# Maxima over partitions through TensorE instead of GpSimd, and dense queries in the two halves of the array

## The chip, the cores and the metric

The kernel runs on one core of one Trainium2 chip. A core has TensorE (PE: matrix products; PEld is its weight load), VectorE (DVE), ScalarE (ACT), GpSimd (POOL) and SyncE (SP, which issues most DMAs). Each engine works through its own queue in order and waits for the others by semaphores. The metric is the device time of one execution in microseconds.

## The reference

Three steps follow each other: attention with a window and four sink positions, a routed layer of eight experts, each of which takes exactly 192 tokens, and a dense two-layer network with a leaky activation.

```python
scores = scale * np.matmul(q, k.transpose(0, 1, 3, 2))     # q, k, v: (2, 8, 768, 64)
keep = is_sink | in_window                                 # 4 sinks, window of 128
scores = np.where(keep, scores, -1000000000.0)
a = np.exp(scores - np.max(scores, axis=-1, keepdims=True))
a = a / (np.sum(a, axis=-1, keepdims=True) + 1e-09)
x = np.matmul(a, v)                                        # then (1536, 512)

logits = x @ w_gate                                        # (1536, 8)
for idx in np.argsort(-logits.flatten()):                  # best pair first
    tok, e = idx // 8, idx % 8
    if assigned[tok] >= 0 or counts[e] >= 192: continue
    assigned[tok] = e; counts[e] += 1
out[assigned == e] = np.maximum(x[assigned == e] @ w1[e], 0.0) @ w2[e]    # w1: (512, 1024)

h = out @ w_in                                             # (1536, 512) @ (512, 2048)
return (np.maximum(h, 0.0) + alpha * np.minimum(h, 0.0)) @ w_out
```

## The kernel before

The program is written as a list of tasks, each with the engines that could do it, an assumed duration, the buffers it reads and writes, and what it must follow. A planner (`Plan.run`) goes through that list in simulated time: of the tasks that could start it takes the one that starts first, by rank where they tie, fixes its engine and takes its buffers from their rings. The order on each engine, and the choice of engine where there are two, come from these assumed durations; the chip only keeps the order. The planner assumes 0.42 or 0.48 us for a reduction over partitions on GpSimd. `boost` raises a task's rank.

**Attention.** Twelve blocks of 128 queries (two batches of six), in each four pairs of heads. `qk` makes the scores of a pair: for each head one product of 128 rows, with the head's 64 rows of queries in a stationary tile whose other 64 rows are zeros (`qT` is laid out that way, 512 KB per block), against the keys of both heads, 130 or 260 columns. The scores go to four banks, the ring `s`. VectorE masks them and takes the row's minimum (`soft`, L451), ScalarE takes the exponential (`expo`, L462), TensorE turns P (`transp`, L476), ScalarE and VectorE split it in two halves of 16 bits (`hilo`, L485, L486), and TensorE multiplies with V (`pv`, L527 to L535), four to seven steps later. V too is split, after it was scaled by a power of two: `vmax` takes the largest |v| of each partition, `vscale` combines the blocks of a batch (L375), and `pow2_scale` takes the maximum over all 128 partitions and makes the scale and its inverse from the exponent bits. The maximum is a `partition_all_reduce` on GpSimd (L356). `pow2_scale` runs three times, for each batch and for the gate's weights. `prep_v` then splits V on GpSimd (`vh` L405, scaled V L407, `vl` L409), for the first block on ScalarE and VectorE.

**Routing.** Eight experts close one after another. `closing` counts, for every pair of token and expert, how many tokens stand ahead of it (masks `cm` on VectorE, ScalarE or GpSimd, L966 to L985; counts on TensorE, L1017). From these `thresholds` finds per partition and expert the key of the last token that fits (`red`, L1031), and `total` takes the maximum over partitions, again a `partition_all_reduce` on GpSimd (`tot`, L1034). `close` (`name`, L896 to L900) picks the expert with the highest key, `ranks` (L1049) numbers its tokens. Seven closings do this; the eighth expert takes what is left. Then one-hot tiles `ohs` (L1114) give the token numbers (L1231), GpSimd gathers the rows by indirect DMA (`xg`, L1250) and TensorE turns them (L1263, 128 and 64 rows in turn).

**Experts and chunks.** Two experts (L1345 to L1352) and then one chunk of the dense network with their 384 tokens (`lay1` L1419, `lay2` L1441), four times over. Operands are split in a high part (`spl`, L1297, and `gt`, L1428, on ScalarE) and a low part (L1288, on GpSimd or VectorE). The dense weights are converted to 32 bits along the way (L765 to L776).

The closings run beside the experts and chunks of the step before. What the change touches most are these lines:

```python
m2 = cst.tile([128, 1], F32, name="m2" + name)
task({"POOL": 0.42}, lambda: nc.gpsimd.partition_all_reduce(m2, m1[0], 128, ...ReduceOp.max), r=[m1[1]], w=[a])   # L356
...
def total():
    nc.gpsimd.partition_all_reduce(tot.tile, red.tile, 128, ...ReduceOp.max)      # L1034
```

## Time and profile before

| | before |
|---|---|
| median of 3 runs | 765.0 us (764.94 to 768.23) |
| profiled execution | 766.29 us, span 764.6 us |
| mean granted TensorE clock | 0.888 |
| busy: PE, PEld | 625.8 us (82%), 547.6 us (72%) |
| busy: DVE, ACT, POOL | 535.1 us (70%), 391.3 us (51%), 398.0 us (52%) |
| DMA | 79.24 MB, mean 104 GB/s |
| reductions over partitions on GpSimd | 3 at L356 (first at 19.8 us), 7 at L1034 (142.5 to 571.3 us) |

In a timeline row stand the start and the length in us, engine, line, operation and tiles, and in brackets how long the engine was idle before it and what ended that; "issue" there means that nothing the profile shows ended it. In a row of the waits stand who waited for whom, the sum in us, the number of times and the longest. PE's time is the time that its instructions are in the array, so that overlapping ones count once.

### The profile page before, as it was taken

The numbers are of one execution on the slowest core, as the hardware profiler recorded it, in microseconds if no ns is written. First come the engines' busy times: TensorE is split into PE (matmuls) and PEld (weight loads), VectorE is DVE, ScalarE is ACT, GpSimd is POOL, SyncE is SP. The second block draws the span as 40 slices with busy tenths as digits, with TensorE's granted clock in tenths as the row PEclk, the third lists the DMA queues.
The fourth block names the chain that finished last, engine by engine and source line by source line (L and its number), as shares of the span: only waits on it lengthen the run. The fifth ranks groups of instructions, "written<-read, shape, count | busy, mean of one in ns | idle before, by whom it ended". The sixth has DMA issues, their size and how long they took to land.

```text
span 764.6 us, 12677 instructions
## 1 busy us (share of the span) xinstructions
PE 625.8 (82%) x4473; PEld 547.6 (72%) x4474; DVE 535.1 (70%) x1225; ACT 391.3 (51%) x865; POOL 398.0 (52%) x425
## 2 busy tenths in 40 slices
PE   5559997749699577768989995949786999989996
PEld 4448886438598466557888874739785988888995
DVE  5548889749577799956888875627964655886651
ACT  6448887324363466324775342317634444775452
POOL 4526744242431566426766654337645556766563
PEclk9579997559889799778999998879998999999998
DMA  8835433515773453102740003016402002730001
GB/s 252 261 97 135 129 72 74 191 51 189 252 252 107 137 166 98 48 28 60 212 157 1 3 22 121 29 48 219 158 1 83 1 22 83 223 122 1 1 1 42
DMA packets 40283, 79.24 MB, mean 104 GB/s; under 512 B 15518, under 2 KB 22204, under 8 KB 40124
## 3 DMA queue, kind: packets, MB, share of 16 engines
q1 hardware_dynamic: 37916, 71.60, 29.9%
q0 software_dynamic: 2304, 6.84, 2.7%
q8 instruction: 35, 0.57, 0.3%
q14 instruction: 28, 0.23, 0.1%
HBM read 69.45 MB, written 6.36 MB: 99 GB/s over the span
## 4 chain that ended last, share of the span: by engine, by line
PE 38%; DVE 24%; issue 10%; ACT 5%; DMA 4%; POOL 3%; POOLq 0%; ACTq 0%; DVEq 0%; SPq 0%
PE o L1441 12%; PE h L1419 12%; DVE cm L970 4%; PE h L1345 4%; DVE spl L1288 3%; DVE ohs L1114 2%; DVE v L1426 2%; PE h L1352 2%; PE r L1263 2%; DVE w L769 2%; ACT spl L1297 2%; DVE h L1337 2%; PE h L1347 2%; DMA xg<-xd,sidx 2%; DMA raw<-w 1%
## 5 line engine op out<-in xcount | busy, mean ns | idle before, releaser
L1441 PE MATMUL o<-spl,gt 128*128 128x512 f32 x576 | 162.0, 425 | 37.6 <-POOL gt L1288 24.0
L1288 POOL TENSOR_TENSOR spl<-w,spl 128x512 fp32r<-128x512 f32 x81 | 113.0, 1399 | 90.1 <-ACT spl L1297 52.3
L1441 PEld LDWEIGHTS o<-spl,gt 128*128 128x128 f32 x576 | 112.5, 203 | 64.3 <-POOL gt L1288 28.0
L1419 PE MATMUL h<-x,spl 128*128 128x384 f32 x768 | 151.7, 348 | 1.7 <-POOL x L1288 0.7
L1419 PEld LDWEIGHTS h<-x,spl 128*128 128x128 f32 x768 | 141.7, 196 | 8.0 <-DVE x L1288 1.2
L1288 POOL TENSOR_TENSOR spl<-raw,spl 128x512 fp32r<-128x512 f32 x57 | 76.2, 1343 | 43.1 <-ACT spl L1297 23.1
L1426 DVE SCALAR_TENSOR_TENSOR v<-t,nal,v 128x384 f32<-128x384 f32 x64 | 70.0, 1094 | 21.5 <-ACT t L1424 20.5
L1288 POOL TENSOR_TENSOR gt<-v,gt 128x384 fp32r<-128x384 f32 x50 | 55.5, 1111 | 46.3 <-ACT gt L1428 39.3
L1297 ACT CAST spl<-w 128x512 fp32r<-128x512 f32 x94 | 57.8, 619 | 33.4 <-PE o L1441 17.7
L1428 ACT CAST gt<-v 128x384 fp32r<-128x384 f32 x64 | 32.8, 513 | 80.5 <-DVE v L1426 79.3
L1345 PE MATMUL h<-xT,spl 128*128 128x384 f32 x192 | 59.2, 373 | 10.5 <-DVE jt L1333 10.5
L1297 ACT CAST spl<-raw 128x512 fp32r<-128x512 f32 x92 | 55.4, 619 | 16.8 <-PE o L1441 6.1
L1288 DVE TENSOR_TENSOR spl<-w,spl 128x512 fp32r<-128x512 f32 x47 | 42.2, 898 | 26.4 <-ACT spl L1297 26.1
L1345 PE MATMUL h<-h,spl 128*128 128x384 f32 x192 | 56.3, 362 | 3.1 <-DVE h L1337 1.7
L1423 ACT ACTIVATE v<-h 128x384 f32<-128x384 f32 x64 | 31.3, 489 | 51.3 <-PE h L1419 45.9
L442 PE MATMUL s<-k,q 128*128 128x260 f32 (+1 forms) x192 | 53.3, 408 | 3.9 <-DMA q<-qT 3.8
L970 DVE TENSOR_SCALAR cm<-mrow,m 128x384 bf16<-128x384 f32 (+10 forms) x85 | 55.2, 685 | 1.6 <-ACT mrow L955 1.6
L1288 DVE TENSOR_TENSOR spl<-raw,spl 128x512 fp32r<-128x512 f32 x39 | 39.8, 1022 | 20.5 <-ACT spl L1297 19.9
L1017 PEld LDWEIGHTS <-cm 128*128 128x128 bf16 x684 | 24.2, 100 | 41.3 <-DVE cm L970 32.6
L462 ACT ACTIVATE P<-sm,mn 128x260 f32<-128x260 f32 (+1 forms) x96 | 43.6, 489 | 11.1 <-DVE mn L451 10.8
L1347 PE MATMUL h<-xT,spl 128*128 128x192 f32 x192 | 49.0, 255 | 0.0
L1347 PE MATMUL h<-h,spl 128*128 128x192 f32 x192 | 48.1, 251 | 0.0
(199 smaller groups left out, 1344.2 us busy)
## 6 DMA issues: line engine op xcount, KB each, us to landing
raw<-w SPq DMA_DIRECT2D x64, 512.0 KB, 3.9
r<-w_in SPq DMA_DIRECT2D x16, 512.0 KB, 3.4
r<-w_out SPq DMA_DIRECT2D x16, 512.0 KB, 3.9
q<-qT SPq DMA_DIRECT2D x11, 512.0 KB, 9.5
vraw<-v SPq DMA_DIRECT2D x4, 768.0 KB, 8.2
xd<-x SPq DMA_DIRECT2D x12, 256.0 KB, 2.4
k<-kT SPq DMA_DIRECT2D x11, 260.0 KB, 4.4
mrow<-md SPq DMA_DIRECT2D x3, 384.0 KB, 3.1
```

Source lines behind the costliest of these rows:

```text
L442: nc.tensor.matmul(s.tile[:, :n], lhsT=qs[t].tile[:, p, a], rhs=kk, start=True, stop=True)
L462: task({"ACT": act(n) + 0.137}, lambda h=h, sm=sm, mn=mn: nc.scalar.activation(P[t].tile[:, h, :n], sm.tile[:, :n], AF.Exp, bias=mn.tile, ...
L970: nc.vector.tensor_scalar(cm.tile[:, x:y], mrow[:, x:y], m.tile[:, c1:c1 + 1], None, op)
L1288: eng.tensor_tensor(*aps(), OP.subtract)
L1297: (nc.scalar.copy if e == "ACT" else nc.vector.tensor_copy)(b.tile[:, 0], get())
L1345: nc.tensor.matmul(ps.tile[:, 0:2 * CAP], lhsT=w[:, 0, k], rhs=x.rearrange("p a t -> p (a t)"), start=first and k == 0, stop=False, skip_g ...
L1347: nc.tensor.matmul(ps.tile[:, CAP:2 * CAP], lhsT=w[:, 1, k], rhs=x[:, 0], start=False, stop=last and k == len(xs) - 1, skip_group_check=True)
L1419: nc.tensor.matmul(ps.tile[:, 0:CH], lhsT=w[:, i, k], rhs=x[:, j], start=(k == n == 0), stop=(k == KD - 1 and n == 2))
L1423: task({"ACT": act(CH)}, lambda: nc.scalar.activation(v.tile, ps.tile[:, 0:CH], AF.Relu), r=[ps], w=[v])
L1426: task({"DVE": dve(CH) + 0.065}, lambda: nc.vector.scalar_tensor_tensor(v.tile, t.tile, nal[:, f:f + 1], v.tile, OP.mult, OP.add), r=[t, n ...
L1428: task({"ACT": act_sb(CH)}, lambda: nc.scalar.copy(gt.tile[:, 0], v.tile), r=[v], w=[gt.part(0)])
L1441: nc.tensor.matmul(ops[t].tile, lhsT=gt.tile[:, i, sl], rhs=wo.tile[:, j], start=(f == n == 0), stop=(f == FB - 1 and n == 2))
```

## The change

Three things are changed.

First, no maximum over partitions is on GpSimd any more. In `pow2_scale` TensorE turns the 128 maxima into one row in a bank of the ring `s`, VectorE takes the row's maximum, TensorE spreads it back over 128 partitions (a transpose of the value repeated 128 times), and the four small operations read it from the bank. These tasks get a `boost` of 40. In `closing` the same is done for eight experts at once: `red` (128 x 8) is turned to 8 x 128 in free columns of the bank that holds the counts, VectorE takes eight maxima (`tot`, now 8 x 1), and a second transpose gives 128 x 8; `close` reads that from the bank.

Second, the queries are dense: `qT` holds the two heads of a pair in partitions 0 to 63 and 64 to 127 and no zeros (256 KB per block), and each head's product takes its own half: 64 rows of queries against 64 rows of keys. Both products of a pair are one task, with two banks.

Third, the planner, asked whether a task with several new buffers of one ring can start, looks for as many free ones (`free_at(n)`).

```diff
-    def free_at(self):
-        return self.pick()[0]
+    def free_at(self, n=0):
+        if not n:
+            return self.pick()[0]
+        at = []
+        for old in self.past:
+            if old is None:
+                at.append(0.0)
+            elif all(t.start is not None for t in old.users):
+                at.append(max((t.end for t in old.users), default=0.0))
+        return sorted(at)[n] if len(at) > n else None
...
-                            f = b.ring.free_at()
+                            f = b.ring.free_at(asked.count(b.ring))
+                            asked.append(b.ring)
...
+EAGER = 40.0
...
-    r_q, r_P = ring("q", [128, NP, 2, 128], F32, 4), ring("P", [128, H, 2 * KW], F32, 2)
+    r_q, r_P = ring("q", [128, NP, 128], F32, 4), ring("P", [128, H, 2 * KW], F32, 2)
...
     def pow2_scale(m1, name):
-        m2 = cst.tile([128, 1], F32, name="m2" + name)
+        m2 = cst.tile([128, 2], F32, name="m2" + name)
         o = cst.tile([128, 4], I32, name="sc" + name)
-        a, b = Res(), Res()
+        a, b, c, ps = Res(), Res(), Res(), r_s.new()
         def power():
-            nc.vector.tensor_scalar(m2, m2, 1.0e-30, None, OP.max)
-            nc.vector.tensor_scalar(o[:, 0:1], m2.bitcast(I32), 0x7F800000, None, OP.bitwise_and)
+            nc.vector.tensor_scalar(m2[:, 0:1], ps.tile[:, 128:129], 1.0e-30, None, OP.max)
+            nc.vector.tensor_scalar(o[:, 0:1], m2[:, 0:1].bitcast(I32), 0x7F800000, None, OP.bitwise_and)
...
-        task({"POOL": 0.42}, lambda: nc.gpsimd.partition_all_reduce(m2, m1[0], 128, bass.bass_isa.ReduceOp.max),
-             r=[m1[1]], w=[a])
-        task({"DVE": 0.6}, power, r=[a], w=[b])
+        task({"PE": 0.12}, lambda: nc.tensor.transpose(ps.tile[0:1, 0:128], m1[0], ident), r=[m1[1]], w=[ps.part(0)], boost=EAGER)
+        task({"DVE": 0.2}, lambda: nc.vector.tensor_reduce(m2[0:1, 1:2], ps.tile[0:1, 0:128], AX.X, OP.max),
+             r=[ps.part(0)], w=[a], boost=EAGER)
+        task({"PE": 0.12}, lambda: nc.tensor.transpose(ps.tile[:, 128:129], m2[0:1, 1:2].to_broadcast([1, 128]), ident[0:1, 0:1]),
+             r=[a], w=[ps.part(1)], boost=EAGER)
+        task({"DVE": 0.6}, power, r=[ps.part(1)], w=[b], boost=EAGER)
...
     def qk(t, p):
         b, i, j0, n = geo(t)
-        for a in range(2):
-            s = S[t, p, a] = r_s.new()
-            def fn(a=a, s=s):
-                kk = kall[:, b, p].rearrange("p j k -> p (j k)")[:, j0 * KW:j0 * KW + n]
-                nc.tensor.matmul(s.tile[:, :n], lhsT=qs[t].tile[:, p, a], rhs=kk, start=True, stop=True)
-            qks.append(pe(n / 599.0 + 0.012, fn, [...], [s]))
+        ss = [r_s.new() for _ in range(2)]
+        S[t, p, 0], S[t, p, 1] = ss
+        def fn():
+            for a, s in enumerate(ss):
+                half = slice(a * D, (a + 1) * D)
+                kk = kall[half, b, p].rearrange("p j k -> p (j k)")[:, j0 * KW:j0 * KW + n]
+                nc.tensor.matmul(s.tile[:, :n], lhsT=qs[t].tile[half, p], rhs=kk, start=True, stop=True)
+        qks.append(pe(n / 599.0 + 0.05, fn, [...], ss))
...
-        self.r_qm, self.r_tot = ring("qm", [128, C, E], F32, 1), ring("tot", [128, E], F32, 1)
+        self.r_qm, self.r_tot = ring("qm", [128, C, E], F32, 1), ring("tot", [E, 1], F32, 1)
...
-        def total():
-            nc.gpsimd.partition_all_reduce(tot.tile, red.tile, 128, bass.bass_isa.ReduceOp.max)
+        def total(x):
+            if x == 0:
+                nc.tensor.transpose(cnt.tile[0:E, 128:256], red.tile, ident)
+            elif x == 1:
+                nc.vector.tensor_reduce(tot.tile, cnt.tile[0:E, 128:256], AX.X, OP.max)
+            else:
+                nc.tensor.transpose(cnt.tile[:, 256:256 + E], tot.tile.to_broadcast([E, 128]), ident[0:E, 0:E])
...
-        seq.append(task({"POOL": 0.48}, total, r=[red], w=[tot]))
+        seq.append(task({"PE": 0.12}, lambda: total(0), r=[red, *counted], w=[cnt.part("t")]))
+        seq.append(task({"DVE": 0.25}, lambda: total(1), r=[cnt.part("t")], w=[tot]))
+        seq.append(task({"PE": 0.12}, lambda: total(2), r=[tot], w=[cnt.part("b")]))
...
-            self.name(ei, sm.tile, mx.tile, tot.tile)
+            self.name(ei, sm.tile, mx.tile, cnt.tile[:, 256:256 + E])
```

The order on the engines changes with it. Line numbers in the new kernel are 11 to 22 higher: L1017 is L1031 there, L1231 L1253, L1288 L1310, L1419 L1441, L1426 L1448, L1441 L1463.

GpSimd in attention's first batch, where the scale of the second batch is made. Before, a reduction `m2v` stands between the V blocks, between two instructions named `ISA` alone, which the profile calls MODIFY_POOL_CONFIG (`vl` is the low part of V, `sk` the sinks' columns of P):

```order
61 L407 TENSOR_SCALAR vraw<-vraw,scv_151 128x512
62 L356 ISA
63 L356 ISA m2v_156<-m_155 128x1
64 L409 ISA
65 L409 TENSOR_TENSOR vl_635<-vraw,vh_320 128x512
66 L495 TENSOR_SCALAR sk_659<-P_557 128x32
```

Now, at the same V block:

```order
57 L421 TENSOR_SCALAR vraw<-vraw,scv_151 128x512
58 L423 TENSOR_TENSOR vl_621<-vraw,vh_329 128x512
59 L513 TENSOR_SCALAR sk_661<-P_496 128x32
60 L514 TENSOR_TENSOR sk_661<-P_496,sk_661 128x32
61 L515 TENSOR_SCALAR sk_661<-P_496 128x32
```

The reduction and both `ISA` rows are gone, and `sk` follows `vl` as before.

GpSimd at the third closing, in the first chunk (`w`: dense weights in conversion, `spl` and `gt`: low parts of weights and activations). Before:

```order
180 L776 TENSOR_TENSOR w_2685<-w_2685,sg_3682 128x512
181 L1034 ISA
182 L1034 ISA tot_3738<-red_3717 128x8
183 L776 ISA
184 L776 TENSOR_TENSOR w_2686<-w_2686,sg_3734 128x512
185 L1288 TENSOR_TENSOR spl_3787<-w_2675,spl_3787 128x512
186 L1288 TENSOR_TENSOR gt_3813<-v_3765,gt_3813 128x384
```

The same closing is now on TensorE, between the products of the chunk (L1463 and L1441; `x3` and `x12` are equal products in a row):

```order
2639 L1031 MATMUL r_3470<-oh_3279,cm_3724 128x8
2640 L1463 MATMUL o_3794<-spl_3174,gt_3781 128x512 x3
2641 L1463 MATMUL o_3802<-spl_3174,gt_3781 128x512 x3
2642 L1050 MATMUL r_3470<-ident,red_3868 8x128
2643 L1463 MATMUL o_3811<-spl_3174,gt_3781 128x512 x3
2644 L1441 MATMUL h_3890<-x_3218,spl_3761 128x384 x12
2645 L1054 MATMUL r_3470<-ident,tot_3888 128x8
```

and on VectorE, from `red` to the first operation of `close` (L910):

```order
582 L1045 TENSOR_REDUCE red_3868<-both_3867 128x8
583 L1059 SCALAR_TENSOR_TENSOR qm_3876<-oh_3279,r_3470 128x96
584 L1310 TENSOR_TENSOR spl_3845<-w_2690,spl_3845 128x512
585 L781 TENSOR_SCALAR w_2701<-w_2701 128x512
586 L1052 TENSOR_REDUCE tot_3888<-r_3470 8x1
587 L783 SCALAR_TENSOR_TENSOR w_2701<-r_3754,w_2701 128x512
588 L781 TENSOR_SCALAR w_2702<-w_2702 128x512
589 L1310 TENSOR_TENSOR spl_3904<-w_2693,spl_3904 128x512
590 L783 SCALAR_TENSOR_TENSOR w_2702<-r_3786,w_2702 128x512
591 L781 TENSOR_SCALAR w_2703<-w_2703 128x512
592 L910 TENSOR_REDUCE mx_3923<-r_3470 128x1
```

Two operations of other work stand ahead of the maximum and five between it and `close`, and fifteen products between the two transposes.

More of the change, by code (lines that the diff above doesn't have):

```diff
@@ L150, in run @@
                 for t in c:
-                    s = max(at, t.est[e])
+                    s, asked = max(at, t.est[e]), []
                     for b in t.bufs:
                         if b.tile is None:
-                            f = b.ring.free_at()
+                            f = b.ring.free_at(asked.count(b.ring))
+                            asked.append(b.ring)
                             if f is None:
@@ L286, in load_q @@
         q = qs[t] = r_q.new()
-        load(lambda: nc.sync.dma_start(out=q.tile, in_=qT[block(t)]), [q], 4 * 128 * NP * 256)
+        load(lambda: nc.sync.dma_start(out=q.tile, in_=qT[block(t)]), [q], 4 * 128 * NP * 128)
     def load_v(a, b):
@@ L295, in attention @@
         load(lambda p=p: nc.sync.dma_start(out=kall[:, 0, p, 0], in_=kT[0][:, p]), [k0_res[p]], 4 * 128 * KW)
-        load(lambda p=p: nc.sync.dma_start(out=q0.tile[:, p], in_=qT[0][:, p]), [q0.part(p)], 4 * 128 * 256)
+        load(lambda p=p: nc.sync.dma_start(out=q0.tile[:, p], in_=qT[0][:, p]), [q0.part(p)], 4 * 128 * 128)
     def load_w():
@@ L436, in qk @@
         b, i, j0, n = geo(t)
-        for a in range(2):
-            s = S[t, p, a] = r_s.new()
-            def fn(a=a, s=s):
-                kk = kall[:, b, p].rearrange("p j k -> p (j k)")[:, j0 * KW:j0 * KW + n]
-                nc.tensor.matmul(s.tile[:, :n], lhsT=qs[t].tile[:, p, a], rhs=kk, start=True, stop=True)
-            qks.append(pe(n / 599.0 + 0.012, fn, [qs[t].part(p) if t == 0 else qs[t], *([k0_res[p]] if b * NB + j0 == 0 else []), *k_res[b * NB + j0:b * NB + i + 1]], [s]))
+        ss = [r_s.new() for _ in range(2)]
[5 more added lines that the diff above has]
+                nc.tensor.matmul(s.tile[:, :n], lhsT=qs[t].tile[half, p], rhs=kk, start=True, stop=True)
+        qks.append(pe(n / 599.0 + 0.05, fn, [qs[t].part(p) if t == 0 else qs[t], *([k0_res[p]] if b * NB + j0 == 0 else []),
+                                             *k_res[b * NB + j0:b * NB + i + 1]], ss))
     def soft(t, p, a):
@@ L673, in lay_out_attention @@
     a = {}
-    qT = np.zeros((B, NB, 2, D, NP, 2, 128), q.dtype)
-    qt = q.reshape(B, NP, 2, NB, 128, D).transpose(0, 3, 2, 5, 1, 4)
-    for x in range(2):
-        qT[:, :, x, :, :, x] = qt[:, :, x]
-    a["qT"] = qT.reshape(NBLK, 128, NP, 2, 128)
+    a["qT"] = np.ascontiguousarray(q.reshape(B, NP, 2, NB, 128, D).transpose(0, 3, 2, 5, 1, 4)).reshape(NBLK, 128, NP, 128)
     kt = k.reshape(B, NP, 2, NB, 128, D).transpose(0, 3, 2, 5, 1, 4)
@@ L1050, in ranks @@
             nc.vector.tensor_reduce(rk.tile[:, 0:nb], rf.tile[:, 0:nb], AX.X, OP.add)
-        seq.append(task({"DVE": 0.9}, close, r=[tot], w=[sm, mx, ei]))
+        seq.append(task({"DVE": 0.9}, close, r=[cnt.part("b")], w=[sm, mx, ei]))
         seq.append(task({"DVE": 0.15 + 2 * dve(nb * E)}, ranks, r=[qm, sm], w=[rf, rk]))
```

## The prediction

> **What bounds the kernel now.** I read the page's busy line and chain first, then busy time by stage, then the waits of the engines that stand still.
>
> ```profile
> PE 38%; DVE 24%; issue 10%; ACT 5%; DMA 4%; POOL 3%; POOLq 0%; ACTq 0%; DVEq 0%; SPq 0%
> 0.00:60.00 60.00, 34.61 (x224) 28.76 (x225) 31.60 (x131) 29.74 (x69) 25.74 (x69) 0.72 0.62 194
> 60.00:120.00 60.00, 58.93 (x777) 51.91 (x776) 52.81 (x208) 51.93 (x122) 33.75 (x61) 0.99 0.48 116
> 120.00:165.00 45.00, 24.56 (x288) 18.05 (x289) 32.00 (x109) 18.95 (x32) 17.21 (x19) 0.60 0.36 111
> 165.00:350.00 185.00, 144.45 (x1078) 124.37 (x1078) 146.28 (x298) 86.57 (x171) 82.94 (x66) 0.86 0.41 138
> 350.00:600.00 250.00, 209.81 (x1264) 186.41 (x1263) 170.85 (x338) 119.82 (x282) 142.09 (x126) 0.91 0.26 83
> 600.00:765.00 165.00, 153.42 (x847) 138.11 (x845) 101.57 (x145) 84.27 (x192) 96.29 (x87) 0.99 0.19 57
> ```
>
> The stage rows give stretch, length, busy time of PE, PEld, DVE, ACT and POOL, then granted clock, DMA share and GB/s. TensorE is full only in two stretches: 58.93 of 60 us in the steady part of attention, 153.42 of 165 at the end. In the first 60 us it works 34.61, between 165 and 600 us 354 of 435. So the time is TensorE's work plus holes, and in the chain a tenth is "issue", time that no work explains. Its places are on GpSimd:
>
> ```profile
> 19.82 0.38 POOL L356 PARTITION_ALL_REDUCE m2w<-m1w  x1 [9.28 <-issue]
> 27.99 1.36 POOL L405 TENSOR_SCALAR vh<-vraw,scv 128x512 f16<-128x512 f32 x2 [7.46 <-ACT junk L367]
> 45.11 0.38 POOL L356 PARTITION_ALL_REDUCE m2v<-m  x1 [6.71 <-issue]
> 52.56 1.11 POOL L409 TENSOR_TENSOR vl<-vraw,vh 128x512 f16<-128x512 f32 x1 [7.08 <-issue]
> 160.53 1.79 POOL L977 TENSOR_SCALAR cm<-mrow,m 128x128 bf16<-128x128 f32 x2 [6.96 <-issue]
> 331.90 0.39 POOL L1034 PARTITION_ALL_REDUCE tot<-red  x1 [5.91 <-issue]
> 339.22 0.98 POOL L1288 TENSOR_TENSOR gt<-v,gt 128x384 fp32r<-128x384 f32 x1 [6.93 <-issue]
> 500.74 0.39 POOL L1034 PARTITION_ALL_REDUCE tot<-red  x1 [6.66 <-issue]
> 507.81 1.25 POOL L1288 TENSOR_TENSOR spl<-raw,spl 128x512 fp32r<-128x512 f32 x1 [6.68 <-issue]
> 198.87 1.52 POOL L1250 DMA_INDIRECT xg<-xd,sidx  x1 [0.18 <-DVE far L1036]
> ```
>
> The reduction itself takes 0.39 us. But the engine stands still 5.9 to 9.3 us ahead of it and 6.7 to 7.5 us behind it, where the next ordinary operation follows; the pair of L1034 and L1288 at 331.90 and 339.22 costs 13.2 us of GpSimd for 0.39 us of work. An indirect DMA between ordinary operations costs no such pause (last row, 0.18). This is a change of code on the engine, both ways; ten reductions make nine episodes, since two stand side by side. It matters because of who waits:
>
> ```profile
> DVE mx L896 <- POOL tot L1034: 25.8, 6, 5.8
> 21.96 1.97 PE L476 MATMUL pt<-ident,P 128*128 128x128 f32 x8 [4.23 <-DVE ptl L486]
> 31.82 0.21 PE L529 MATMUL pv<-vl,pth 128*128 128x64 f16 x1 [2.88 <-POOL vl L409]
> 47.20 0.99 PE L476 MATMUL pt<-ident,P 128*128 128x128 f32 x4 [3.85 <-DVE ptl L486]
> 54.44 0.34 PE L504 MATMUL pv<-identh,sk 128*96 128x128 f16 x1 [4.51 <-POOL sk L497]
> 163.69 0.21 PE L1017 MATMUL r<-oh,cm 128*128 128x8 bf16 x2 [10.22 <-DVE cm L970]
> 255.87 1.22 PE L1441 MATMUL o<-spl,gt 128*128 128x512 f32 x2 [8.33 <-ACT gt L1428]
> 334.74 1.47 PE L1231 MATMUL r<-tok,ohs 128*128 128x1 f16 x16 [2.62 <-DVE ohs L1114]
> 340.25 0.79 PE L1441 MATMUL o<-spl,gt 128*128 128x512 f32 x1 [2.98 <-POOL gt L1288]
> 349.20 1.20 PE L1441 MATMUL o<-spl,gt 128*128 128x512 f32 x4 [2.45 <-POOL gt L1288]
> 464.40 1.63 PE L1231 MATMUL r<-tok,ohs 128*128 128x1 f16 x12 [4.49 <-DVE ohs L1114]
> 477.80 0.45 PE L1263 MATMUL r<-ident,xg 128*128 128x128 f32 x1 [3.47 <-DMA xg<-xd,sidx]
> 510.07 0.80 PE L1441 MATMUL o<-spl,gt 128*128 128x512 f32 x1 [10.57 <-POOL gt L1288]
> 581.35 2.93 PE L1441 MATMUL o<-spl,gt 128*128 128x512 f32 x6 [5.08 <-POOL gt L1288]
> 205.62 0.34 PE L1263 MATMUL r<-ident,xg 64*128 64x64 f32 x1 [6.21 <-DMA xg<-xd,sidx]
> ```
>
> The bracket is TensorE's idle time and who ended it. VectorE stands at `mx` until the reduction is through, the low parts `gt` and `spl` stand in GpSimd's queue until its code is back, and TensorE runs dry at each place but the last row, 205.62, where a gather lands late and no code change is in the way.
>
> **Term 1, the start of attention: -18 us.** Removed: three reductions, two episodes. Behind the first, GpSimd's work on V begins at 27.99 and TensorE has its first `vl` at 31.82. The new way to the scale is two transposes, a short reduction and the four small operations that stood there before:
>
> ```profile
> 16.01 0.16 DVE L375 TENSOR_REDUCE m<-mx 128x1 f32<-128x6 f32 x1
> 21.17 0.14 DVE L354 TENSOR_SCALAR scv<-scv 128x1 int32<-128x1 int32 x1
> 465.96 0.38 PE L935 MATMUL r<-ident,m 128*6 128x128 f32 x1
> ```
>
> By L935, two transposes are 0.8 us; with 0.2 for the reduction and 0.6 for the four operations the scale comes 1.7 us after the maximum, near 18.0 instead of 21.3. GpSimd then starts at about 18 instead of 28: -10 at the first `vl`. Behind the second episode TensorE's holes 3.85 and 4.51 fall together with VectorE's, -8.4. Upper bound: the clock of 0.72 in the first 60 us returns to the 0.99 of the next stretch, and 34.61 us of work shrink by 9 more, -27. Lower bound: the loads bind next (DMA share 0.62), and half remains, -9. I stay at -18, the sum of the holes, since loads shrink too: the query transfers are halved (12 blocks, 256 instead of 512 KB, 3 MB at 194 GB/s is 16 us of transfer). I give that no credit of its own; the V loads that cover it set the scale's time, and they come at most 2 us earlier. The new wait is TensorE's, for the maxima of VectorE; behind it in TensorE's queue stand transposes of P and the first products with V, which could not have run before the scale anyway. The two transposes borrow one of the four `s` banks of the scores for some 2 us; the idle time of TensorE ahead of 21.96 covers that, and if it is gone, one pair of scores starts that much later.
>
> **Term 2, dense queries: +2 us.** The two products of a pair of heads, each over 128 rows with half zeros, become two over 64 rows each, in different halves of the array.
>
> ```profile
> 115.92 0.45 PE s L442 x4
> 116.85 0.44 PE pt L476 x4
> 640.51 1.85 PE r L1263 x8
> ```
>
> A pair of 130 columns takes 0.45 us (x4: each product has two records), so one of 260 about 0.90. Nothing here shows two products side by side, so I bound it. The change of height has a price in the trace: L1263 turns 128 and 64 rows alternately, 0.23 us each, while equal transposes (L476) take 0.11: 0.12 to 0.15 us per change, two changes per pair, 0.30. No overlap: 0.90 + 0.30 = 1.20. Full overlap: 0.45 + 0.30 = 0.75. I take the middle, 0.98, which is also what comes out if the records keep their order: the second of the first head runs beside the first of the second, three steps of four. Of 48 pairs about 27 wide ones lie in the full stretch from 60 to 120 us: 27 x 0.08 = +2, ends -4 and +8. Below -7 it cannot go there, as VectorE has 52.81 us of work in these 60.
>
> The Trainium skill has a rule on either side here. Its page "TensorEngine Tiling (Array Packing)", section Theoretical Speedup, allows up to 2x for a contraction of 64; the section Key Properties says that a change of tiling mode drains the engine. By the first alone the pair would be 0.45 us and the term 27 x -0.45 = -12; no run here shows it. With the second the trace agrees (0.23 against 0.11 us at L1263 and L476), and by it, without overlap, the term would be the +8 above.
>
> **Term 3, the seven closings of routing: -44 us.** In each, L1034 becomes a transpose, a VectorE maximum over 8 rows and a transpose back: by L935 about 0.8 us and 0.2, with hand-overs some 1.2 us instead of 0.39, cover by the other VectorE work that now stands between (in the order, up to five operations). The new wait is VectorE's for TensorE, whose queue has one to fifteen products between the two transposes; TensorE waits for `red` in turn. What goes, hole by hole, less what stays late next (the counts, the gathered rows, the chain itself): first closing 10.22, less 2 as the gather lands, -8; second, no hole of this cause, 0; third 8.33, -8; fourth 2.62 + 2.98 + 2.45, -7; fifth 4.49 + 3.47, -6; sixth 10.57, -10; seventh 5.08, -5. Sum -44. Lower bound -22: VectorE has 146.28 of 185 us between 165 and 350, so the holes may refill. Upper bound -58: clocks of 0.86 and 0.91 go to 0.99, worth 10 to 15 us of TensorE's own work.
>
> The planner's own correction (`free_at` asked for the n-th free buffer) only counts the two `s` buffers that a pair now takes together: 0.
>
> **Sum.** The profiled execution took 766.3 us, of which 764.6 are span: 766.3 - 18 + 2 - 44 = 706. The median shown is 765.0, 1.3 less, so 705. As a check: behind what is now 165 us it leaves 600 - 36 = 564 us for TensorE's 508 us of work there (the last three stage rows), a share of 90%, between the 84% of 350 to 600 and the 93% of the end.
>
> **Rivals.** *Half is taken back.* VectorE becomes the bound from 165 to 350, loads at the start: -9 + 2 - 22 gives 736 at worst, midway to the forecast is about 725. For it: VectorE's share there equals TensorE's. Against: VectorE itself stands 25.8 us at `mx`. *Both halves overlap and the clock returns:* -4, -25 and -52, 684. For it: the clock figures above; against: the drain price. *Slower:* the transposes tie VectorE to TensorE's in-order queue; a closing then costs a whole round of product, `v`, `gt` and product, about 6 us by the rows of these steps. The gain of term 3 would go, not of term 1: 745. It decides from 9 us more per closing than now (60 over 7); at 10 the time is 775, and no row here has a round that long without a code change in it. *The code changes stay,* because something else on GpSimd calls for them: then only term 2 and the waits for the sum remain, 763; the gap of 0.18 at the indirect DMA speaks against.
>
> By the 2x of the Trainium skill's page on tiling alone, without a drain, the time would be 691, and its chance lies in that of the second rival.
>
> **Chances.** Forecast (695 to 718) 0.52; half taken back (718 to 745) 0.22; overlap and clock (676 to 695) 0.20; slower 0.03; code changes stay 0.03. The range 686 to 732 holds the first and most of the next two. Half a per cent, 4 us, is about what can be told from no change: faster 0.94, same 0.03, slower 0.03.
>
> **What would show it.** No reduction on GpSimd and no idle of 6 us there by "issue"; `mx` waits under 2 us each; first `vl` used near 22 us, last score products near 100 us instead of 116; PE's holes at the third and sixth closing under 2 us; score records of 64 rows, whose second head starts with or after the first's end, tells overlap. Wrong if TensorE waits at L1050 or L1054 for several us, or if VectorE is over 95% busy between 150 and 330 us.

## The result and the profile after

The changed kernel takes 689.0 us (median, 688.2 to 691.0) where the kernel before took 765.9 in the same comparison: a ratio of 0.900 with a 95% interval of 0.897 to 0.903, 77 us less. The forecast of 705 had 60. The time lies inside the range of 686 to 732, but only 3 us from its lower end: the forecast itself had given 695 to 718, and 689 is in the stretch of the second rival ("both halves overlap and the clock returns", 676 to 695). The profiled execution took 688.23 us, 686.5 of them span.

First the chain and the stage rows of the kernel after, in the same form as before (stretch, length, busy time of PE, PEld, DVE, ACT and POOL, granted clock, DMA share, GB/s):

```profile
PE 46%; DVE 28%; issue 8%; DMA 8%; ACT 5%; POOL 3%; SPq 1%; POOLq 0%; DVEq 0%; ACTq 0%
0.00:60.00 60.00, 46.16 (x459) 32.00 (x459) 46.75 (x196) 42.57 (x98) 37.87 (x89) 1.00 0.73 197
60.00:120.00 60.00, 49.82 (x751) 38.62 (x750) 56.01 (x210) 48.66 (x110) 32.92 (x51) 0.87 0.40 92
120.00:165.00 45.00, 36.06 (x322) 29.09 (x321) 37.35 (x100) 15.98 (x29) 17.27 (x12) 0.76 0.51 160
165.00:350.00 185.00, 158.51 (x1100) 139.51 (x1099) 164.00 (x304) 106.29 (x226) 105.86 (x84) 0.92 0.48 157
350.00:600.00 250.00, 235.11 (x1460) 208.77 (x1459) 190.09 (x372) 132.94 (x309) 158.34 (x137) 0.98 0.27 84
600.00:686.00 86.00, 78.63 (x412) 71.00 (x411) 48.90 (x65) 40.31 (x89) 47.87 (x42) 0.99 0.05 17
```

In the first 60 us TensorE now works 46 us instead of 35 (the clock of 1.00 in that row can't be trusted; the last section says why); between 165 and 600 it works 394 of 435 instead of 354. In attention VectorE has taken its place as the fullest engine: 56.0 of 60 us in the second row, more than TensorE's 49.8.

The waits that carried the prediction are nearly gone. Of the waits of the kernel after (who waited for whom, sum, times, longest):

```profile
DVE mx L910 <- PE r L1054: 0.6, 1, 0.6
PE o L1463 <- POOL gt L1310: 1.3, 2, 1.1
PEld r L1050 <- DVE qm L1059: 6.3, 3, 5.1
```

VectorE's 25.8 us at `mx` are 1.0, 0.6 in this row and 0.4 at the first closing. The third row is the new wait: TensorE's queue stands at the closing's first transpose until VectorE has `red`. It cost something once, at 226.70. TensorE's rows, first the very first `vl` product of the kernel before, then the kernel after:

```profile
23.80 0.24 PE L529 MATMUL pv<-vl,pth 128*128 128x64 f16 x1
```

```profile
24.40 0.21 PE L547 MATMUL pv<-vl,pth 128*128 128x64 f16 x1 [2.35 <-DVE vl L416]
29.87 0.19 PE L547 MATMUL pv<-vl,pth 128*128 128x64 f16 x1
137.70 0.20 PE L1031 MATMUL r<-oh,cm 128*128 128x8 bf16 x2 [3.20 <-DVE cm L984]
226.70 0.31 PE L1050 MATMUL r<-ident,red 128*8 128x128 f32 x1 [4.65 <-DVE qm L1059]
436.54 0.27 PE L1050 MATMUL r<-ident,red 128*8 128x128 f32 x1
436.57 0.94 PE L1463 MATMUL o<-spl,gt 128*128 128x512 f32 x3
437.44 0.22 PE L1054 MATMUL r<-ident,tot 8*128 8x8 f32 x1
```

The row at 31.82, which the prediction took for the first `vl` product, is that of the second block, whose low part GpSimd makes; its counterpart is the row at 29.87, 2 us earlier. The first block's low part is made on VectorE, and its product runs at 24.40 where it ran at 23.80, a little later. The hole of 10.22 us at the counts behind the first closing is 3.20, and at the sixth closing (last three rows), where TensorE stood 10.57 us, it now works through: both transposes slip between products.

Seen by milestones of the two traces, the kernel after is ahead by 20.9 us at the last product of scores (96.6 instead of 117.5), by 38.7 at the first output product of the first chunk (217.2), by 46.8 at that of the second (366.8), by 75.1 at that of the third (500.4) and by 78.1 at that of the fourth (619.8).

### The profile page after: what moved, and what is told of

Its sections match the earlier page's. It is cut to its first block, busy times and chain, and to the rows that moved or that the text cites. A ratio compares the mean times of both kernels' runs of the same rounds, so it can differ in the third digit from the quotient of the medians.

```text
span 686.5 us, 12683 instructions
## 1 busy us (share of the span) xinstructions
PE 604.3 (88%) x4490; PEld 519.0 (76%) x4491; DVE 543.1 (79%) x1242; ACT 386.7 (56%) x858; POOL 400.1 (58%) x412
## 4 chain that ended last, share of the span: by engine, by line
PE 46%; DVE 28%; issue 8%; DMA 8%; ACT 5%; POOL 3%; SPq 1%; POOLq 0%; DVEq 0%; ACTq 0%
PE h L1441 13%; PE o L1463 12%; PE h L1367 4%; DVE cm L984 4%; PE s L459 3%; DVE spl L1310 3%; PE pt L494 3%; DVE ohs L1136 3%; DMA raw<-w 3%; DVE v L1448 2%; DMA xg<-xd,sidx 2%; PE h L1374 2%; ACT spl L1319 2%; DMA vraw<-v 2%; PE r L1285 2%
## 5 line engine op out<-in xcount | busy, mean ns | idle before, releaser
L1310 POOL TENSOR_TENSOR spl<-w,spl 128x512 fp32r<-128x512 f32 x77 | 109.5, 1424 | 86.4 <-ACT spl L1319 54.0
L1463 PE MATMUL o<-spl,gt 128*128 128x512 f32 x576 | 154.7, 412 | 3.4 <-ACT gt L1450 2.1
L1441 PE MATMUL h<-x,spl 128*128 128x384 f32 x768 | 150.4, 346 | 1.3 <-POOL x L1310 0.7
L1441 PEld LDWEIGHTS h<-x,spl 128*128 128x128 f32 x768 | 140.4, 195 | 7.1 <-DVE x L1310 1.1
L1463 PEld LDWEIGHTS o<-spl,gt 128*128 128x128 f32 x576 | 107.6, 194 | 24.6 <-POOL gt L1310 3.0
L1310 POOL TENSOR_TENSOR spl<-raw,spl 128x512 fp32r<-128x512 f32 x55 | 73.5, 1343 | 37.2 <-ACT spl L1319 26.2
L1310 POOL TENSOR_TENSOR gt<-v,gt 128x384 fp32r<-128x384 f32 x52 | 58.2, 1120 | 42.3 <-ACT gt L1450 42.2
L1448 DVE SCALAR_TENSOR_TENSOR v<-t,nal,v 128x384 f32<-128x384 f32 x64 | 63.9, 999 | 15.7 <-ACT t L1446 15.6
L1310 DVE TENSOR_TENSOR spl<-w,spl 128x512 fp32r<-128x512 f32 x51 | 47.1, 924 | 25.4 <-ACT spl L1319 25.1
L1310 DVE TENSOR_TENSOR spl<-raw,spl 128x512 fp32r<-128x512 f32 x41 | 40.7, 1000 | 17.3 <-ACT spl L1319 16.9
L984 DVE TENSOR_SCALAR cm<-mrow,m 128x384 bf16<-128x384 f32 (+10 forms) x85 | 51.3, 637 | 1.8 <-ACT mrow L969 1.8
L1031 PEld LDWEIGHTS <-cm 128*128 128x128 bf16 x684 | 23.8, 99 | 35.1 <-DVE cm L984 24.5
L1367 PEld LDWEIGHTS h<-xT,spl 128*128 128x128 f32 x192 | 37.1, 193 | 10.6 <-DVE jt L1355 9.3
```

Of the source, the lines that this page charges most:

```text
L984: nc.vector.tensor_scalar(cm.tile[:, x:y], mrow[:, x:y], m.tile[:, c1:c1 + 1], None, op)
L1031: nc.tensor.matmul(v()[:, c], lhsT=cm.tile[:, c * 128:(c + 1) * 128], rhs=oh.tile[:, c1], start=(len(begun) == 1 and c == lo), stop=(len(b ...
L1310: eng.tensor_tensor(*aps(), OP.subtract)
L1367: nc.tensor.matmul(ps.tile[:, 0:2 * CAP], lhsT=w[:, 0, k], rhs=x.rearrange("p a t -> p (a t)"), start=first and k == 0, stop=False, skip_g ...
L1441: nc.tensor.matmul(ps.tile[:, 0:CH], lhsT=w[:, i, k], rhs=x[:, j], start=(k == n == 0), stop=(k == KD - 1 and n == 2))
L1448: task({"DVE": dve(CH) + 0.065}, lambda: nc.vector.scalar_tensor_tensor(v.tile, t.tile, nal[:, f:f + 1], v.tile, OP.mult, OP.add), r=[t, n ...
```

## The experiments

All times are compared by the ratio to the kernel before, run on the same chip in the same comparison. The kernel after stands at 0.8996; a ratio of 0.01 is 7.7 us. A difference of less than about 4 us between two changed kernels can't be told from none.

| kernel | median us | ratio, 95% interval | against after |
|---|---|---|---|
| after without dense queries | 692.4 | 0.903 (0.898 to 0.908) | +3 |
| after, scale's maxima on GpSimd | 707.9 | 0.923 (0.917 to 0.928) | +18 |
| after, closings' totals on GpSimd | 749.2 | 0.977 (0.972 to 0.983) | +60 |
| before with dense queries alone | 765.1 | 0.997 (0.994 to 0.999) | |
| after, plus seven unread GpSimd totals | 740.5 | 0.966 (0.962 to 0.970) | +51 |
| totals on GpSimd, planner told 13.5 us | 719.8 | 0.939 (0.933 to 0.945) | +30 |
| after, both heads in one half | 730.2 | 0.952 (0.949 to 0.955) | +40 |
| after, boost for the closing's steps | 705.3 | 0.917 (0.914 to 0.921) | +14 |
| after, no boost for the scale's steps | 693.0 | 0.900 (0.896 to 0.904) | 0 |
| after, closing's rank lowered | 690.8 | 0.899 (0.895 to 0.903) | -1 |
| after, planner's threshold 1.15 | 700.1 | 0.912 (0.908 to 0.915) | +9 |
| after, planner told a pair's true time | 687.0 | 0.895 (0.891 to 0.899) | -4 |

### The three parts, undone one at a time

**Dense queries.** The zero-padded `qT` and the two separate products return:

```diff
-                half = slice(a * D, (a + 1) * D)
-                kk = kall[half, b, p]...
-                nc.tensor.matmul(s.tile[:, :n], lhsT=qs[t].tile[half, p], rhs=kk, ...)
+                kk = kall[:, b, p]...
+                nc.tensor.matmul(s.tile[:, :n], lhsT=qs[t].tile[:, p, a], rhs=kk, ...)
```

> The new kernel (689) with the zero-padded queries of before, two separate tasks for a pair. Theory: the dense pair is cheaper, about 0.64 us in the new trace against 0.90, so undoing it costs about 27 wide pairs x 0.26 = 7: 697 (694 to 702), with score products of 0.45 per wide head again. By the prediction's term (dense costs 2) it would be 687. Rival: VectorE holds attention's steady part anyway (19.39 of 20 us at 60 to 80): 689, no change.

It took 3 us more, with an interval that reaches to none. In TensorE's timeline of the kernel after, and then of this one, four transposes, a pair of 260 columns and the next operation behind it:

```profile
80.95 0.60 PE L494 MATMUL pt<-ident,P 128*128 128x128 f32 x4
81.48 0.71 PE L459 MATMUL s<-k,q 64*128 64x260 f32 x4
82.12 0.26 PE L522 MATMUL pv<-identh,sk 128*96 128x128 f16 x1
```

```profile
72.58 0.60 PE L490 MATMUL pt<-ident,P 128*128 128x128 f32 x4
73.01 1.04 PE L456 MATMUL s<-k,q 128*128 128x260 f32 x4
73.89 0.19 PE L541 MATMUL pv<-vh,pth 128*128 128x65 f16 x1
```

From start to start a dense pair takes 0.64 us, a zero-padded one 0.88 (0.96 behind some operations). The four records of the dense pair start two by two, 6 to 7 ns apart: the two halves run fully side by side. But each change of height costs something that the zero-padded pair doesn't pay. The dense pair starts 0.20 us after the last transpose instead of 0.11, and its first two records and its last two take 0.32 us each until the next start, where 0.22 is usual inside a row of pairs: together 0.29. So from the transposes to the operation behind the pair it is 1.17 us instead of 1.31, 0.14 less and not 0.24. For 27 pairs that is 4 us, and up to the last score product TensorE's busy time is indeed 81.7 us instead of 85.5. The kernel has some 3 of these 4.

**The kernel before with dense queries alone** (all ten reductions on GpSimd, and `free_at(n)`, which stays in every kernel here with a pair in one task and was not undone by itself):

> The kernel before with dense queries alone, all ten reductions on GpSimd. Theory: the start is set by the scale and its code changes, so of the 7 us of shorter score products some 4 remain: 761 (756 to 765). Rival 1: the halved loads and the shorter products count in full or more: 750. Rival 2: VectorE holds attention: 765, no change. If the sum of the three parts undone one at a time is well below 77, they lean on each other.

It gained 0.3% (0.1 to 0.6%), 2.5 us: less than the theory's 4 and more than nothing. The dense queries are worth 2 to 3 us with or without the rest.

**The maxima of the scale** go back to GpSimd:

```diff
-        task({"PE": 0.12}, lambda: nc.tensor.transpose(ps.tile[0:1, 0:128], m1[0], ident), ...)
-        ... maximum on VectorE, transpose back
+        task({"POOL": 0.42}, lambda: nc.gpsimd.partition_all_reduce(m2, m1[0], 128, ...), r=[m1[1]], w=[a])
```

> The new kernel with the three maxima of the scale back on GpSimd. Theory (the prediction's term 1): its two code changes return, first vl product near 30 instead of 23 and holes of some 4 us at the second batch's scale, 689 + 18 = 707 (701 to 711). Rival: the loads hold the start, so only half is lost: 698.

18 us, as the theory had it; that only half is lost, as the loads would have it, is excluded. GpSimd's rows of this kernel, then of the kernel after at the same place:

```profile
19.88 0.38 POOL L367 PARTITION_ALL_REDUCE m2v<-m  x1 [9.32 <-issue]
20.18 0.42 POOL L367 PARTITION_ALL_REDUCE m2w<-m1w  x1
28.11 1.36 POOL L416 TENSOR_SCALAR vh<-vraw,scv 128x512 f16<-128x512 f32 x2 [7.51 <-ACT x L598]
```

```profile
21.11 1.37 POOL L419 TENSOR_SCALAR vh<-vraw,scv 128x512 f16<-128x512 f32 x2 [10.82 <-DVE scv L365]
```

Both maxima are out by 20.6 on GpSimd, and the scale follows at 20.9; through TensorE it is there at 21.1, no sooner. It is the 7.51 us behind the reduction that make GpSimd's work on V wait until 28.11 instead of 21.11. The last score product comes at 113.8 instead of 96.6. Of these 17.2 us, 10.7 are idle time of TensorE (25.6 instead of 14.9 up to there), and 6.5 are the same products at a slower pace (88.2 us busy instead of 81.7): products with V start 54 ns apart between 72 and 89 us, where they start 29 to 30 apart in the kernel after.

**The totals of the seven closings** go back to GpSimd:

```diff
-        seq.append(task({"PE": 0.12}, lambda: total(0), r=[red, *counted], w=[cnt.part("t")]))
-        seq.append(task({"DVE": 0.25}, lambda: total(1), r=[cnt.part("t")], w=[tot]))
-        seq.append(task({"PE": 0.12}, lambda: total(2), r=[tot], w=[cnt.part("b")]))
+        seq.append(task({"POOL": 0.48}, total, r=[red], w=[tot]))
```

> The new kernel with the seven totals of the closings back on GpSimd. Theory (the prediction's term 3, with the larger gain seen): 689 + 47 = 736 (728 to 745), waits of VectorE at mx of about 25 us in sum again, chunks' gaps of 5 to 10 us at PE back at the third and sixth closing. Rival (most of the gain came from the earlier start and denser attention): 711 or less.

It took 60 us more, beyond the theory's 47. Its waits show the old picture, and TensorE's output products, grouped (busy time, mean ns of one, idle time ahead of them), show a second thing; the last row is that of the kernel after:

```profile
DVE mx L910 <- POOL tot L1048: 26.1, 6, 6.0
PE o L1455 <- POOL gt L1302: 26.1, 8, 11.0
L1455 PE MATMUL o<-spl,gt 128*128 128x512 f32 x576 | 163.8, 428 | 42.3 <-POOL gt L1302 26.1 <-ACT gt L1442 14.9 <-DVE gt L1302 1.2
```

```profile
L1463 PE MATMUL o<-spl,gt 128*128 128x512 f32 x576 | 154.7, 412 | 3.4 <-ACT gt L1450 2.1 <-POOL gt L1310 1.3
```

The idle time ahead of these products goes from 42.3 to 3.4 us, and the same 576 products are 9.1 us shorter. By TensorE's holes of over 1.5 us in the two traces, 19 of them (80.5 us) became 12 (28.7). So 52 us of the 60 are holes, and most of the rest is the same work done more slowly: TensorE is busy for 613.7 us instead of 604.3. How much of these 9 is the clock after a hole is less certain: behind the last score product TensorE's busy time varies by 7 us among the kernels that leave the closings on TensorE as they are. The sum of the three parts, 3 + 18 + 60, is 81 for 77 together: they hardly lean on each other.

### Was it the latency of the maximum, or the code change on GpSimd?

Two theories remain for the 60 us. By one, VectorE and the routing chain waited for the total; by the other, whatever stood behind the reduction in GpSimd's queue waited for its code. The next kernel keeps the closing on TensorE and adds the old reduction, which nobody reads:

```diff
+        spare = self.r_gp.new()
+        task({"POOL": 0.48}, lambda: nc.gpsimd.partition_all_reduce(spare.tile, red.tile, 128, ...), r=[red], w=[spare])
         seq.append(task({"PE": 0.12}, lambda: total(0), r=[red, *counted], w=[cnt.part("t")]))
```

> The new kernel plus, in each of the seven closings, the old reduction on GpSimd, whose result nobody reads; the closing itself still goes through TensorE. Theory A (GpSimd's code change blocks its queue: low parts gt and spl and the gathers stand behind it): most of the 60 us that the closings were worth comes back, 730 or more. Theory B (VectorE's wait for the total at mx, and the routing chain behind it, was the price): at most 12 come back, 701 or less. Between, 701 to 730, both count, in the ratio of the distances from 689 and 749.

51 of the 60 us came back, though the total itself comes as fast as in the kernel after: from `red` to `mx` the seven closings take 20.5 us in sum, 21.7 in the kernel after and 31.1 with the totals on GpSimd. GpSimd's rows at the first closing and at the fourth, and then TensorE's behind each:

```profile
120.88 0.40 POOL L1063 PARTITION_ALL_REDUCE gp<-red  x1 [5.72 <-DVE red L1046]
128.61 2.82 POOL L1276 DMA_INDIRECT xg<-xd,sidx  x1 [7.33 <-DMA raw<-w]
139.65 1.79 POOL L992 TENSOR_SCALAR cm<-mrow,m 128x128 bf16<-128x128 f32 x2 [7.01 <-issue]
...
313.42 0.39 POOL L1063 PARTITION_ALL_REDUCE gp<-red  x1 [5.82 <-DVE mx L913]
320.98 1.25 POOL L1314 TENSOR_TENSOR spl<-w,spl 128x512 fp32r<-128x512 f32 x1 [7.16 <-issue]
```

```profile
142.81 0.22 PE L1032 MATMUL r<-oh,cm 128*128 128x8 bf16 x2 [10.27 <-DVE cm L985]
...
322.29 1.97 PE L1445 MATMUL h<-x,spl 128*128 128x384 f32 x5 [7.02 <-POOL spl L1314]
```

This is the mechanism in a few rows. For 0.4 us of work GpSimd stands still 5.7 us ahead of it and 7.0 to 7.2 behind it, before its first ordinary operation (the 7.33 ahead of the gather are another wait, for the token numbers, which VectorE has ready at 127.7); the mask `cm` or the low part `spl` that stands there comes late, and TensorE stands 10.27 and 7.02 us. Nobody needs the result, and it costs 51 us all the same. What is left for the latency of the maximum is some 9 us, with an uncertainty of about 5. By the Trainium skill's "GPSIMD Engine Reference", section 2.1 Instruction dispatch, the first call to newly loaded code pays about 6 us, with no instruction in the profile that shows it; the rows agree ahead of the reduction (5.72, 5.82) and show that the way back has a price as well (7.01, 7.16).

If the price is the queue, an order made with the true price should avoid part of it. The totals are on GpSimd, but the planner assumes 13.5 us:

```diff
-        seq.append(task({"POOL": 0.48}, total, r=[red], w=[tot]))
+        seq.append(task({"POOL": 13.5}, total, r=[red], w=[tot]))
```

> The new kernel with the seven totals back on GpSimd as in the run with 749, but the planner assumes 13.5 us for each instead of 0.48, the reduction with a code change on either side. Theory: the planner moves low parts and gathers to VectorE or ahead of the reduction, half of the 60 us is saved: 720 (708 to 735). Rival (a closing's chain cannot be shortened by order, the total still comes 6 us late): 745 or more.

Half of the 60 us is saved, as the theory expected. At the first closing it comes at a price, as GpSimd's rows and then TensorE's show:

```profile
122.87 0.39 POOL L1048 PARTITION_ALL_REDUCE tot<-red  x1 [6.01 <-DVE qm L1053]
143.12 2.82 POOL L1264 DMA_INDIRECT xg<-xd,sidx  x1 [19.86 <-issue]
```

```profile
123.48 15.81 PE L1215 MATMUL r<-ones 128*128 128x512 bf16 x62 [0.22 <-issue]
```

The kernel fills idle time that the planner foresees on TensorE with products of ones that nobody reads. For a total of 13.5 us it puts 62 of them here, where the kernel with the cheap assumption has 4, and they stand ahead of the products that make the token numbers; the gather waits for these. The first chunk's output begins 11.5 us later than with the cheap assumption (248.3 instead of 236.8), the third 27 earlier (531.8 instead of 558.8). So an order made with the true price wins back about half of what the reductions cost, even with this fill against it; what a better order could win was not tried.

### Does a pair gain by the overlap?

Both heads' products use rows 0 to 63, so that they can't run beside each other. The second head gets the first one's scores:

```diff
-                half = slice(a * D, (a + 1) * D)
+                half = slice(0, D)
```

> The new kernel with both heads' products of a pair in the same half of the array (rows 0 to 63), so the second head gets the first one's scores; loads and order unchanged. Theory (the two halves run side by side): now they cannot, a wide pair goes from about 0.64 to 0.9 us, and TensorE's busy time in attention grows by some 7 to 10 us; time 692 (690 to 696) as with zero-padded queries. Rival (the halved loads, not the overlap, gave the 3 us): 689.

Both expectations missed: it took 40 us more. TensorE's rows of this kernel early, and later in attention:

```profile
81.80 0.24 PE L545 MATMUL pv<-vh,pth 128*128 128x65 f16 x1
81.85 0.25 PE L547 MATMUL pv<-vl,pth 128*128 128x64 f16 x1
...
82.46 2.10 PE L459 MATMUL s<-k,q 64*128 64x260 f32 x4
84.49 0.34 PE L522 MATMUL pv<-identh,sk 128*96 128x128 f16 x1
...
104.39 1.14 PE L459 MATMUL s<-k,q 64*128 64x260 f32 x4
105.46 0.66 PE L494 MATMUL pt<-ident,P 128*128 128x128 f32 x4
```

Later a pair takes 1.07 us from start to start (0.97 where two follow each other), and the dense one 0.64. That settles the question: with the same loads, the same order and the same changes of height, the overlap is worth 0.43 us of a pair, two of its four records. But early the same pair takes 2.03 us. The products with V, which the edit does not touch, start 0.05 us apart there; in the kernel after, at that stage, they start 0.03 apart:

```profile
71.00 0.20 PE L545 MATMUL pv<-vh,pth 128*128 128x65 f16 x1
71.04 0.19 PE L547 MATMUL pv<-vl,pth 128*128 128x64 f16 x1
```

All of TensorE runs at half pace. By the median step between products with V in stretches of 5 us, it does so until about 87 us in this kernel (53 to 55 ns, then 29), and until about 29 us in the kernel after. That is where the 40 us are: the last score product comes at 137.4 instead of 96.6.

### Boosts and costs of the planner

**A boost of 40 for the closing's three steps and for `close`:**

```diff
-        seq.append(task({"DVE": 0.9}, close, r=[cnt.part("b")], w=[sm, mx, ei]))
+        seq.append(task({"DVE": 0.9}, close, r=[cnt.part("b")], w=[sm, mx, ei], boost=EAGER))
```

(and so for the three steps of the maximum).

> The new kernel with a boost of 40 for the three steps of a closing's maximum and for close. From red to ei it now takes 2.2 to 6.1 us; with rank ahead of products and low parts it should be about 2 us each, 15 us less in sum. Theory (the closings' chain still sets chunks' starts at the third and fourth): 689 - 5 = 684. Rival (cover by other work, the chain is slack): 689 within 2, or worse by the products that now wait.

Missed: 14 us more. The closings do come earlier (`red` of the third at 187.6 instead of 226.2, of the fifth at 360.5 instead of 408.6), but the boost raises the rank of all that leads to them too, and the chunks' products wait: the first chunk's output begins at 244.1 instead of 217.2. By this the closings had slack, and their maximum is no longer on the path that matters.

**No boost for the steps of the scale** (`EAGER = 0`):

> The new kernel with EAGER = 0: the four steps of each scale have no boost, and a group of transposes of P stands between the scale's steps on TensorE. Theory (the gain of term 1 is the code change, not the boost): 689 to 692, first vl product within 2 us of 23. Rival (the boost counts): 695 or more.

No difference that can be measured: the median is 1 us above the theory's range, the ratio that of the kernel after, and the times spread from 690 to 700. The gain at the start is not the boost's.

**The closing's rank lowered** (`boost=-20` for its first transpose):

> The new kernel with the rank of a closing's first transpose, and so of what leads to it, lowered by 20. A boost of 40 had cost 16 us, by bringing the closings forward and the chunk's products back. Theory (the rank as it is stands near the best, closings have slack at the later experts only): 686 to 694. Rival (lower is better): 684 or less.

No difference, though the third closing's `red` comes at 238.5 instead of 226.2; this too says that the closings have slack. **The threshold for giving a GpSimd task to VectorE** from 0.85 to 1.15 us:

> The new kernel with the planner's threshold for giving a GpSimd task to VectorE raised from 0.85 to 1.15 us, which moves 23 of the low parts from VectorE to GpSimd. Theory (VectorE, 164 of 185 us busy between 165 and 350, is next in line, and GpSimd has room since it no longer changes its code): about 15 us of VectorE's work goes, TensorE gains a part, 685 (682 to 688). Rival (GpSimd takes 1.4 us for a part that VectorE does in 0.9, and TensorE waits for the later part): 691 or more.

Missed: 9 us more. VectorE's busy time falls from 543 to 514 us and GpSimd's rises from 400 to 430, as meant, but TensorE gains nothing. A low part of a dense weight takes 1.42 us on GpSimd and 0.92 on VectorE in the kernel after, and the second chunk's output begins 6 us later, the third's 11. Which of the late parts does it was not settled.

**The planner told 0.64 us for a dense pair** instead of 0.48:

```diff
-        qks.append(pe(n / 599.0 + 0.05, fn, ...
+        qks.append(pe(n / 464.0 + 0.08, fn, ...
```

> The new kernel with the planner told what a dense pair takes on the chip (0.64 us for 260 columns instead of 0.48). Theory: VectorE fills attention (19.4 of 20 us), order hardly moves: 689 within 3. Rival: a truer cost gives a better order in attention: 684 or less.

687.0 us, the shortest of all, but the 4 us less than the kernel after are no more than the uncertainty of comparing the two. None of the versions beats the kernel after clearly.

## Why the prediction was right, and where it was not

**What bounds the kernel: right.** The idle time of 6 to 9 us on GpSimd around a reduction was paid both ways, and the work behind it in GpSimd's queue was what TensorE waited for. The run with the unread reductions shows this by itself. That the engine loads code there is not seen directly; what the traces show is the idle time and the MODIFY_POOL_CONFIG rows beside it, 38 in the kernel before and 2 in the kernel after.

**Term 1, the start, -18: right in size, in part by luck.** Undone, it is 18, where I had 18 of holes; by the traces it is 10.7 of idle time and 6.5 of pace, and the clock I had kept for the upper bound. The first piece, -10 at the first `vl` product, is the step that failed. I took 31.82 for that product, and it is the second block's; it came to 29.87, not 22, and the first block's product didn't gain at all. The scale, forecast for 18.0, is there at 21.1 in the trace. The maximum is ready 1.6 us later than before, as the last piece of V lands later, and from there it takes 3.2 us instead of 1.7, as eight transposes of P (1.94 us) stand between the two transposes in TensorE's queue. GpSimd does begin on V 6.9 us earlier, for want of the code change. The second piece, -8.4 at the second batch's scale, came: neither hole is there in the kernel after. As to the clock: before, products with V were 54 to 55 ns apart, half pace, from 23 to 34 us and again from 54 to 58; now they are so at 24 to 26 us alone, and at 29 ns from 29 us on.

**Term 2, dense queries, +2: it is -2 to -3; the step that failed is the middle.** I took 0.98 us for a pair between bounds of 1.20 (no overlap) and 0.75 (full overlap). The overlap is full. With the later start counted, a pair costs 0.64 + 0.09 = 0.73 us, the lower bound, and the 0.30 that I charged for two changes of height measures 0.29. So the bound of -4 was the term to take: the records start two by two, where I had three steps for four. The Trainium skill's page "TensorEngine Tiling (Array Packing)", section Theoretical Speedup, gives up to 2x for a contraction of 64; that is what the records do here (two start every 0.22 us instead of one), but a pair alone goes from 0.88 to 0.73, 1.2x.

**Term 3, the closings, -44: the mechanism right, the size too small; it is -60, at or past the bound of -58.** For the holes that I listed, the sum came out. With the totals on GpSimd they are 52.2 us; of those over 1.5 us, 7.9 stay in the kernel after (3.20 behind the first closing, 4.65 at the third), so 44 go, and the allowance of 6 for what stays late was about right. Two steps failed. First, I counted these holes alone, and the others fell by some 7 us more. One is at the second closing, which I put at nothing, as a gather lands late there and no code change is in the way. GpSimd's rows, before and then after, say otherwise:

```profile
197.42 1.27 POOL L1288 TENSOR_TENSOR spl<-w,spl 128x512 fp32r<-128x512 f32 x1 [9.25 <-ACT mrow L955]
```

```profile
162.58 1.27 POOL L1310 TENSOR_TENSOR spl<-w,spl 128x512 fp32r<-128x512 f32 x1 [9.67 <-ACT spl L1319]
169.66 1.48 POOL L1272 DMA_INDIRECT xg<-xd,sidx  x1 [5.81 <-DVE x L1389]
```

Before, the token numbers are ready at 194.8, but the gather goes out at 198.87, behind a low part that itself comes 9.25 us after the reduction. After, they are ready at 169.4 and it goes out at 169.66. TensorE's hole of 6.2 us becomes two of 2.2, and with the unread reductions it is 7.5.

Second, I kept the clock for the upper bound, and it came: some 9 us by these two traces. Both show best between the first output products of the second and the third chunk, where the fifth and sixth closing lie. The row of the kernel after, and then of the kernel with the totals on GpSimd:

```profile
366.80:500.40 133.60, 123.20 (x809) 108.28 (x809) 108.13 (x222) 69.32 (x161) 85.86 (x74) 0.97 0.27 86
```

```profile
395.40:558.80 163.40, 129.91 (x830) 114.08 (x828) 107.81 (x239) 68.96 (x161) 84.50 (x76) 0.91 0.23 71
```

The stretch is 29.8 us shorter: TensorE idles 10.4 us instead of 33.5, and works 123.2 instead of 129.9, at a clock of 0.97 instead of 0.91. I had 16 for these two closings and 28 for the other five; by the same milestones, those are worth 32, close to the forecast.

**The gap as a whole.** The forecast was 16 us too long, and the clock in terms 1 and 3 (6.5 and 9) is as much. The other errors, less idle time won at the start than forecast, more at the closings, and the pair, nearly cancel. That the time fell inside the range, 3 us from its end, is owed to the range's width.

**The new waits: bounded rightly.** TensorE waits for `red` at L1050 for 6.3 us over three closings, 5.1 of it at the third. I had called "several us" at L1050 a sign that the forecast is wrong, and TensorE's holes at the third and sixth closing under 2 us a sign that it is right; the third, with 4.65, failed both, and one such wait did not decide it. The sign "no idle of 6 us by issue" on GpSimd is not sharp either: 13.4 us of it remain ahead of the first gather (130.34), with no reduction near, and the gather waits there for its token numbers. VectorE is at most 56.0 of 60 us busy, in attention, and 164 of 185 between 165 and 350.

**The rivals.** The second one was nearest, in mechanism too: both halves do overlap and the clock did return. Of its terms the overlap was -3 where it had -4, the start -18 where it had -25, and the closings -60 where it had -52. "Half is taken back" had VectorE as the bound between 165 and 350; it is 89% busy there and TensorE 86%, and the holes stayed closed. Three of their prices were added up wrongly: midway between 736 and 705 is about 721, the forecast without the gain of term 3 is 749, and +2 on 765 is 767 and not 763. "Slower" had its price in the right place, TensorE's in-order queue, and it came to some 6 us in all instead of 9 per closing.

## What to carry to other kernels

An operation that makes an engine change its code costs the queue on both sides of it, here 13 us for 0.4 us of work; its own row shows only the 0.4, so look at the idle time ahead of it and ahead of the next ordinary operation, and at who waits there. When you count what such holes are worth, follow also what stands one place further back in that queue (here a gather, 4 us late behind a low part), and give the slower clock behind the holes a share in the forecast and not in its bound alone. And when two short products can run side by side, price the changes of height beside them: here the overlap was full, worth 0.43 us of a pair, and 0.29 of it went into the changes.

## What the runs showed that I had not expected

With both heads in one half of the array, TensorE stayed at half pace for a long time although it was hardly ever idle. Three stretches of that kernel (same form as above):

```profile
60.00:64.00 4.00, 4.00 (x22) 2.56 (x21) 1.54 (x8) 1.61 (x3) 0.56 (x1) 1.00 0.01 1
80.00:84.00 4.00, 4.00 (x23) 2.77 (x21) 0.29 (x1) 0.58 (x1) 1.63 (x4) 1.00 0.00 0
100.00:104.00 4.00, 3.31 (x56) 2.78 (x55) 2.65 (x10) 1.40 (x4) 2.13 (x5) 1.00 0.00 0
```

TensorE is busy 4.00 of 4 us in the first two and has 22 and 23 instructions in them; in the third it has 56 in 3.31. The Trainium skill's page "TensorE: Matmul & The Clock Gate", Part 1, says that the array reaches its full rate after about 3.4 us of sustained work. Here TensorE was over 95% busy from 40 us on and stayed at half rate until about 87, with half of the rows in use; that the rows in use are what counts is my reading, and no run tested it alone. It can't be the whole of it, since from 88 us on the same pairs run at the full rate. The granted clock in these rows says 1.00 from the start, while the pace of the products says half: where no change of the clock has been recorded yet, the row can't be trusted, and the step between equal products tells more. The kernel after has the same 1.00 in its first 60 us and runs at half pace to about 29.
